# V loaded by whole batches in 32 KB descriptors, one ring of five buffers, and V's products over 128 columns of weights

## The chip, the core and the metric

The kernel runs on one core of one Trainium2 chip. The metric is the device time of one execution in microseconds (us), as the median of several executions. A profiled execution gives the trace from which the views below are taken; its span begins with the program's first instruction and ends with its last. The engines are PE (TensorE, matrix products; PEld is its loading of weights), DVE (VectorE), ACT (ScalarE), POOL (GpSimd) and SP (SyncE, which here only issues transfers). Transfers are executed by sixteen DMA engines.

## What is computed

One decoding step: a layer norm of x (8 rows of 512), attention of 32 query heads over 8 key/value heads with a window of the last 2048 keys of the caches, its output projection, and a gate from a small gated unit on the same normed rows.

```python
B, Sq, D = 8, 1, 512
Hq, Hkv, Sk, Dh = 32, 8, 8192, 128
W = min(4096, max(256, Sk // 4))                 # 2048
xn = _layernorm(x, axis=-1)
q = (xn @ wq) -> [B, Hq, 1, Dh]
k, v = the last W rows of the caches, each head serving 4 query heads
p = softmax(q @ k * Dh ** -0.5)
s = (p @ v) -> [B, Sq, Hq * Dh] @ wo
h = sigmoid(xn @ w_gate) * (xn @ w_up)           # F = 1792
return x + s * silu(h @ w_down)
```

All tensors are bf16. K and V windows have 33.5 MB each, wq and wo 4.2 MB each, the three unit weights 5.5 MB: 81 MB, of which each byte is used once.

## The kernel before

**Stages.** The query projection comes first. Then K is read in eight tiles of 4 MB (4 batches by 8 heads by 4 runs of keys make 128 partitions of 32 KB; two sets of four batches, four tiles each). VectorE transposes each K tile in place in eight pieces (L464, `k_turn`), PE makes the scores (L479, `qk`), VectorE takes row maxima (L493), ScalarE the exponentials (L507). For each set of four batches the probabilities are transposed in 32x32 blocks (L527, `soft_turn`) and spread by products with a 0/1 matrix `spread` to the partitions in which V lies (L540, `soft_spread`). VectorE then multiplies them by a 0/1 column per head (L561, `soft_mask`), so that a weight column holds only the probabilities of its own head. V's products (L609, `pv`) accumulate in PSUM; ScalarE copies the sums out (L623) and PE adds up four column groups with the 0/1 matrix `Sel` (L635, `pv_sum`), after which VectorE divides by the denominators (L644). The end is `o_rows` (L657, L664), the unit's last product `unit_out` (L381), wo's products (L723), two VectorE steps and the store.

**V.** A V tile is half a batch: 4 heads by 32 runs of 64 keys, 16 KB per partition, 2 MB, sixteen tiles. The weights of one product are 4 heads x 4 query heads x 4 column groups = 64 columns, and two products stand side by side in the two column halves of the array (`tile_position=(0, w * c)`). A tile has 16 products of 512 columns each.

**Order.** The program's order on every engine is written out by hand (`manual_schedule`). The loop at L669 runs over slots t: eight slots per K tile (piece t is transposed in slot t, its scores are in slot t+4), and from slot `PV_LAG` = 52 on V's products, four slots per V tile, beside the last K tiles' scores. `MASK_AT` sets the slots of the masks; `EXP_AT` those of the exponentials.

**Loads.** All large loads are issued from SP in one order, `loads` (L202): K0 to K6, V0, V1, K7, V2 to V13, gate and up weights, V14, V15, down weights, wo. K tiles and weights lie in a ring of 3 buffers of 32 KB per partition, V tiles in one of 4 buffers of 16 KB. A load waits for the release of its buffer, and `issue_loads` (L216) keeps the order, so that a load that waits holds up all behind it. Each transfer also waits for the completion of the eighth transfer before it, whose semaphore it uses again. wo is loaded in six pieces, so that its products can begin before it is complete.

Of the kernel before, what the change touches and what calls it, by code (L numbers as in the profile page):

```python
# [10 lines left out]
def kernel(  # L11
# [13 lines left out]
    nc = tc.nc  # L25
# [18 lines left out]
    PP = P // GL  # L44
    CH = W // PP
    NQ = P // 32
    NJ = 4
    CC = CH // NJ
    NT = B * NG
# [11 lines left out]
    VSET = NT // HB  # L61
# [14 lines left out]
    NCH = 4  # L76
    KRING = 3
    VRING = 4
    CG = CH // NCH
# [17 lines left out]
    kring = ctx.enter_context(tc.tile_pool(name="kring", bufs=KRING))  # L97
    vring = ctx.enter_context(tc.tile_pool(name="vring", bufs=VRING))
# [19 lines left out]
    def k_tile(shape, name):  # L118
        return kring.tile(shape, bf16, name=name, tag="kring", align_bytes=ALIGN)

    def v_tile(shape, name):
        return vring.tile(shape, bf16, name=name, tag="vring", align_bytes=ALIGN)
# [8 lines left out]
    wq_sb = k_tile([P, KT, Hq * Dh], "wq_sb")  # L131
# [8 lines left out]
    def load_k(i):  # L140
        hb, kq = divmod(i, NK)
        t = k_tile([P, KC, Dh], "k_sb")
# [9 lines left out]
    def v_of(i):  # L152
        hb, n = divmod(i, VSET)
        gg, q = divmod(n, NQ)
        return NQ * hb + q, gg
# [15 lines left out]
    def load_gate_up():  # L171
        t = k_tile([P, 2, KT, F], "wgu_sb")
        for n, w in enumerate((B_w_gate, B_w_up)):
            load(t[:, n], w.rearrange("(p kt) n -> p kt n", kt=KT))
            wgu_sb.append(t[:, n])

    def load_down():
        t = k_tile([P, FT, D], "wd_sb")
# [6 lines left out]
    def load_wo():  # L185
        t = k_tile([P, KW, D], "wo_sb")
# [56 lines left out]
    x_f = ppool.tile([B, D], f32, name="x_f", tag="pp")  # L243
    nc.vector.tensor_copy(out=x_f[:], in_=x_bf[:])  # L244
    stats = work.tile([B, nc.vector.BN_STATS_DIM], f32, name="stats")
    nc.vector.bn_stats(out=stats[:], in_=x_f[:])
    mv = work.tile([B, nc.vector.BN_AGGR_DIM], f32, name="mv")
    nc.vector.bn_aggr(out=mv[:], in_=stats[:])
    eps_t = work.tile([B, 1], f32, name="eps_t")
    nc.vector.memset(eps_t[:], 1e-5)  # L250
    rstd = work.tile([B, 1], f32, name="rstd")
# [19 lines left out]
    for c in range(NCOL):  # L271
# [32 lines left out]
    Hm = consts.tile([P, GL], f32, name="Hm")  # L304
    nc.vector.tensor_reduce(
        out=Hm[:],
        in_=ident[:].rearrange("p (a gl) -> p gl a", gl=GL),
# [3 lines left out]

    spread = consts.tile([P, NG, 2, PP, GL], bf16, name="spread")
    nc.gpsimd.memset(spread[:].rearrange("p a b c d -> p (a b c d)").bitcast(f32), 0.0)
    for j in range(GL):
        for gg in range(NG):
            g = NG * gg + j // 2
            nc.gpsimd.tensor_copy(
                out=spread[:, gg, j % 2, :, j], in_=ident[:, 32 * g : 32 * g + PP]
            )

    w = NCH * GL * rep
    rows_of = ppool.tile([P, w], f32, name="rows_of", tag="pp")
    nc.vector.tensor_reduce(
        out=rows_of[:],
        in_=ident[:].rearrange("p (a m) -> p m a", m=w),
        axis=AX.X,
        op=ALU.add,
    )
    Sel = consts.tile([P, NCH, GL, rep], f32, name="Sel")
    nc.vector.tensor_copy(  # L330
        out=Sel[:], in_=rows_of[:].rearrange("p (g c r) -> p c g r", g=GL, c=NCH)
    )

    NE = P // Hq
    pick = consts.tile([32 * NG, NE, P], bf16, name="pick")
    nc.gpsimd.memset(pick[:].rearrange("p e m -> p (e m)").bitcast(f32), 0.0)
    for gg in range(NG):
        rows = slice(32 * gg, 32 * (gg + 1))
        cols = slice(NE * GL * rep * gg, NE * GL * rep * (gg + 1))
        for e in range(NE):  # L340
            nc.gpsimd.tensor_copy(
                out=pick[rows, e, cols].rearrange("p (h d) -> p h d", d=NE)[:, :, e],
                in_=ident[rows, 32 * gg : 32 * gg + GL * rep],
            )
# [108 lines left out]
    o_sb = work.tile([32 * NG, B, Dh], bf16, name="o_sb")  # L453
    nc.vector.memzero(o_sb[:])
# [76 lines left out]
    def soft_spread(hb):  # L531

        pt = pt_of.pop(hb)[:].rearrange("p c (y m) -> p c y m", y=2)
        pc = ppool.tile([P, NG, NQ, CH, rep], bf16, name="pc_bf", tag="pp")
        for gg in range(NG):
            for ch in range(2):
                c = slice(CB * ch, CB * (ch + 1))
                pT_ps = psum_a.tile([P, CB, NQ, rep], f32, name="pT_ps", tag="acc_ps")
                for y in range(2):
                    nc.tensor.matmul(  # L540
                        pT_ps[:],
                        lhsT=spread[:, gg, y].rearrange("p k g -> p (k g)"),
# [4 lines left out]
                    )  # L547
                nc.scalar.copy(  # L548
                    out=pc[:, gg, :, c, :].rearrange("p q c r -> p c q r"),
# [4 lines left out]
    def soft_mask(hb, gg):  # L554

        pT_of[hb, gg] = work2.tile(
            [P, NQ * CG, GL, NCH * rep], bf16, name="pT_sb"
        )
        pc = pc_of[hb][:, gg].rearrange("p q (c e) r -> p (q c) (e r)", e=NCH)
        for gl in range(GL):  # L560
            nc.vector.tensor_scalar(  # L561
                out=pT_of[hb, gg][:, :, gl, :],
                in0=pc,
                scalar1=Hm[:, gl : gl + 1],
# [3 lines left out]

    GW = GL * rep

    def soft_den(hb):
# [8 lines left out]
        den_ps = psum1.tile([32 * NG, NQ], f32, name="den_ps", tag="misc")  # L580
        rden = small.tile([32 * NG, NQ], f32, name="rden")
        for gg in range(NG):
            rows = slice(32 * gg, 32 * gg + GW)
            nc.tensor.matmul(  # L584
                den_ps[rows, :],
                lhsT=HR[:, GL * gg : GL * (gg + 1)].rearrange("m h r -> m (h r)"),
                rhs=dq[:],
                start=True,
                stop=True,
                tile_position=(0, 32 * gg),  # L590
                skip_group_check=True,
            )
            nc.vector.reciprocal(out=rden[rows, :], in_=den_ps[rows, :])
        rden_of[hb] = rden

    def pv(t):


        i, j = divmod(t, NJ)
        b, gg = v_of(i)  # L600
        w = GL * rep * NCH
        if j == 0:
            acc_tiles[i] = psum_a.tile([P, NCH * Dh], f32, name="acc_ps", tag="acc_ps")
        q = b % NQ
        pT = pT_of[b // NQ, gg][:, CG * q : CG * (q + 1)].rearrange("p c g n -> p (c g n)")
        for n in range(CC // NCH):
            c = n % (P // w)
            ch = CC * j + NCH * n
            nc.tensor.matmul(  # L609
                acc_tiles[i][w * c : w * (c + 1), :],  # L610
                lhsT=pT[:, GL * rep * ch : GL * rep * ch + w],
                rhs=v_tiles[i][:, ch : ch + NCH, :].rearrange("p c d -> p (c d)"),
                start=(j == 0 and n < P // w),
                stop=(j == NJ - 1 and n >= CC // NCH - P // w),
                tile_position=(0, w * c),
                skip_group_check=True,
            )
        if j == NJ - 1:
            if i % NSUM == 0:
                acc_sbs[i // NSUM] = work.tile(  # L620
# [3 lines left out]
                out=acc_sbs[i // NSUM][:, i % NSUM], in_=acc_tiles.pop(i)[:]  # L624
            )

    def pv_sum(i, n):

        b, gg = v_of(i)
        q = b % NQ  # L630
        acc_sb = acc_sbs[i // NSUM][:, i % NSUM : i % NSUM + n]
        rows = slice(32 * gg, 32 * gg + GW)
        o_ps = psum1.tile([32 * NG, NSUM, Dh], f32, name="o_ps", tag="misc")
        for c in range(NCH):
            nc.tensor.matmul(  # L635
                o_ps[rows, :n, :],
                lhsT=Sel[:, c].rearrange("p g r -> p (g r)"),
# [3 lines left out]
                tile_position=(0, 32 * gg),  # L641
# [3 lines left out]
            out=o_sb[rows, b : b + n, :],  # L645
            in0=o_ps[rows, :n, :],
            in1=rden_of[b // NQ][rows, q : q + n].unsqueeze(2).to_broadcast([GW, n, Dh]),
# [21 lines left out]
    for t in range(PV_LAG + NSLOT):  # L669
# [3 lines left out]
        for hb in range(HB):  # L673
            if t == EXP_AT[hb]:
                soft_exp(hb)
            for gg in range(NG):
                if t == MASK_AT[hb, gg]:
                    soft_mask(hb, gg)
# [9 lines left out]
        if u >= NJ and u % NJ == 0:  # L688
            i = u // NJ - 1
            if i == NT - 2:  # L690
# [81 lines left out]
```

## Time and profile before

| | us |
|---|---|
| median of three executions | 197.33 |
| the executions | 197.10, 197.33, 197.42 |
| profiled execution | 197.29 |
| its span | 195.5 |

| engine | busy us | share of the span | instructions |
|---|---|---|---|
| PE | 102.9 | 53% | 750 |
| DVE | 105.5 | 54% | 149 |
| ACT | 30.8 | 16% | 69 |
| POOL | 4.6 | 2% | 25 |

| group | count | mean ns |
|---|---|---|
| L464 DVE transpose of K, 128x1024 | 64 | 1210 |
| L479 PE scores, 512 columns | 256 | 565 |
| L609 PE V's products, 512 columns | 256 | 443 |
| L561 DVE mask, 128x1024 | 16 | 477 |
| L540 PE spread, 512 columns | 16 | 501 |
| L635 PE sums of V's column groups | 48 | 477 |

How to read it: the profile's page lists the busy time of each engine, the same in 40 slices of the span (each digit is tenths), the clock that TensorE was granted (PEclk), the mean busy share of the sixteen DMA engines and the GB/s that they moved; the chain of waits, followed back from the last instruction; and groups of instructions by line and shape. Matrix products are pipelined and their ends are modelled, so the spacing of their starts says more than their length. The trace also holds each DMA packet with its size and time.

### The profile page before, as it was taken

How to read it: one execution, taken by the hardware profiler on the slowest of the kernel's cores; microseconds unless marked ns; L12 is line 12 of the kernel's file. 1: busy time of each engine (PE TensorE's matmuls, PEld its weight loads, DVE VectorE, ACT ScalarE, POOL GpSimd, SP SyncE). 2: the span in 40 equal slices, each digit the busy share in tenths (PEclk: the TensorE clock that was granted, in tenths of full speed). 3: DMA queues.
4: the chain of work that ended last, by engine and by line, in shares of the span. 5: the costliest groups of instructions: out<-in, count | busy, mean ns of one | idle time of the engine just before them, and what ended most of it. 6: DMA issues, size and time to landing. Idle time of an engine off the chain costs nothing.

```text
span 195.5 us, 1888 instructions
## 1 busy us (share of the span) xinstructions
PE 102.9 (53%) x750; PEld 36.2 (19%) x750; DVE 105.5 (54%) x149; ACT 30.8 (16%) x69; POOL 4.6 (2%) x25
## 2 busy tenths in 40 slices
PE   0062014434323258403695989858944893577763
PEld 0020001101000012100121222322311131223551
DVE  0156499999899998899969726403100010040301
ACT  2025050000000084000011143511111114010100
POOL 8000000000000000000000000000000000000000
PEclk9999999999999999955588799988999798597999
DMA  7999999999999999999999999999999999999990
GB/s 276 423 476 429 436 429 429 429 429 421 429 429 429 429 429 429 389 432 463 429 419 432 436 422 429 427 429 429 429 429 432 429 431 425 431 429 432 425 390 30
DMA packets 5128, 81.14 MB, mean 415 GB/s; under 512 B 616, under 2 KB 896, under 8 KB 1152
## 3 DMA queue, kind: packets, MB, share of 16 engines
q1 hardware_dynamic: 5056, 81.01, 97.0%
q8 instruction: 6, 0.10, 0.2%
q10 hardware_dynamic: 64, 0.01, 0.0%
q14 instruction: 2, 0.02, 0.0%
HBM read 81.01 MB, written 0.01 MB: 414 GB/s over the span
## 4 chain that ended last, share of the span: by engine, by line
DMA 62%; DVE 23%; PE 10%; issue 1%; ACT 1%; SPq 0%; DVEq 0%
DMA k_sb<-in_A_k_cache_dram 31%; DMA v_sb<-in_A_v_cache_dram 22%; DVE k_sb L464 18%; DMA wo_sb<-in_A_wo_dram 10%; PE acc_ps L609 4%; DVE pt_bf L527 2%; PE s_ps L479 2%; PE pT_ps L540 2%; PE o_ps L635 2%; DVE mx L493 1%; SPq L116 0%; DVE qz_sb L434 0%; DVE o_sb L644 0%; PE den_ps L584 0%; DVE qT_sb L424 0%
## 5 line engine op out<-in xcount | busy, mean ns | idle before, releaser
L464 DVE STREAM_TRANSPOSE k_sb<-k_sb 128x1024 f32<-128x1024 f32 x64 | 73.7, 1210 | 6.7 <-DMA k_sb<-in_A_k_cache_dram 6.6
L479 PE MATMUL s_ps<-k_sb,qz_sb 128*32 128x512 bf16 x256 | 29.8, 565 | 54.2 <-DVE k_sb L464 48.4
L609 PE MATMUL acc_ps<-v_sb,pT_sb 128*64 128x512 bf16 x256 | 39.6, 443 | 10.7 <-DMA v_sb<-in_A_v_cache_dram 10.6
L644 DVE TENSOR_TENSOR o_sb<-o_ps,rden 16x512 bf16<-16x512 f32 (+2 forms) x6 | 3.0, 504 | 47.5 <-PE o_ps L635 47.5
L479 PEld LDWEIGHTS <-qz_sb 128*32 128x32 bf16 x256 | 8.5, 116 | 78.6 <-issue 55.3
L623 ACT COPY acc_sb<-acc_ps 128x512 f32<-128x512 f32 x16 | 9.4, 586 | 84.7 <-PE acc_ps L609 84.7
L609 PEld LDWEIGHTS <-pT_sb 128*64 128x64 bf16 x256 | 13.3, 120 | 31.5 <-DMA v_sb<-in_A_v_cache_dram 14.6
L635 PE MATMUL o_ps<-acc_sb,Sel 128*16 128x512 f32 (+2 forms) x48 | 15.9, 477 | 3.4 <-ACT acc_sb L623 3.4
L561 DVE TENSOR_SCALAR pT_sb<-pc_bf,Hm 128x1024 bf16<-128x1024 bf16 x16 | 6.6, 477 | 6.7 <-PE acc_ps L609 6.7
L507 ACT ACT_TABLE_LOAD x1 | 1.3, 1283 | 39.9 <-DVE nm L501 39.9
L635 PEld LDWEIGHTS o_ps<-acc_sb,Sel 128*16 128x16 f32 x48 | 4.5, 103 | 14.9 <-issue 7.7
L493 DVE TENSOR_REDUCE mx<-s_ps 128x1 f32<-128x512 f32 x8 | 5.3, 662 | 3.2 <-PE s_ps L479 3.2
L540 PE MATMUL pT_ps<-pt_bf,spread 128*128 128x512 bf16 x16 | 6.0, 501 | 1.3 <-DVE pt_bf L527 0.7
L267 PE MATMUL xnT_ps<-ident,xn_bf 8*128 8x8 bf16 x4 | 0.3, 174 | 11.6 <-DVE xn_bf L257 11.6
L436 ACT COPY qz_sb<-qT_sb 32x32 bf16<-32x32 bf16 x20 | 4.8, 241 | 8.2 <-DVE qT_sb L424 7.9
L355 PE MATMUL d_ps<-wgu_sb,xnT_sb 128*32 128x448 bf16 x32 | 3.0, 511 | 5.3 <-DMA wgu_sb<-in_B_w_up_dram 3.0
L723 PE MATMUL a_ps<-wo_sb,o_sb 128*32 128x256 bf16 x64 | 4.5, 273 | 2.0 <-DMA wo_sb<-in_A_wo_dram 2.0
L507 ACT ACTIVATE p_bf<-s_ps,nm 128x512 bf16<-128x512 f32 x8 | 5.4, 686 | 0.0
L244 DVE CAST x_f<-x_bf 8x512 f32<-8x512 bf16 x1 | 0.4, 415 | 9.2 <-DMA x_bf<-in_A_x_dram 9.2
L548 ACT CAST pc_bf<-pT_ps 128x512 bf16<-128x512 f32 x8 | 4.5, 587 | 5.0 <-DVE pt_bf L527 2.8
L527 DVE STREAM_TRANSPOSE pt_bf<-p_bf 128x512 bf16<-128x512 bf16 x8 | 4.9, 668 | 0.0
L723 PEld LDWEIGHTS <-o_sb 128*32 128x32 bf16 x64 | 3.5, 96 | 3.1 <-issue 3.0
(59 smaller groups left out, 39.4 us busy)
## 6 DMA issues: line engine op xcount, KB each, us to landing
k_sb<-in_A_k_cache_dram SPq DMA_DIRECT2D x8, 4096.0 KB, 19.3
v_sb<-in_A_v_cache_dram SPq DMA_DIRECT2D x16, 2048.0 KB, 15.7
wq_sb<-in_A_wq_dram SPq DMA_DIRECT2D x1, 3072.0 KB, 11.4
wo_sb<-in_A_wo_dram SPq DMA_DIRECT2D x1, 2048.0 KB
wgu_sb<-in_B_w_gate_dram SPq DMA_DIRECT2D x1, 1792.0 KB
wgu_sb<-in_B_w_up_dram SPq DMA_DIRECT2D x1, 1792.0 KB, 24.7
wd_sb<-in_B_w_down_dram SPq DMA_DIRECT2D x1, 1792.0 KB
wq_sb<-in_A_wq_dram SPq DMA_DIRECT2D x1, 1024.0 KB, 4.6
```

What stands on the lines that cost most here:

```text
L436: nc.scalar.copy(out=out, in_=in_)
L464: nc.vector.transpose(out=kw, in_=kw)
L479: nc.tensor.matmul(s_tiles[i][32 * g : 32 * (g + 1), :], lhsT=qz_sb[:, hb, h, 2 * a + e, :], rhs=kT[:, :, a, h, :, e], start=(n == 0), sto ...
L493: nc.vector.reduce_max(out=mx_of[hb][:, kq : kq + 1], in_=s_tiles[i][:], axis=AX.X)
L507: nc.scalar.activation(out=p_bf[:, :, kq], in_=s_tiles.pop(NK * hb + kq)[:].rearrange("p (o c j) -> p c j o", o=2, j=NC), func=AF.Exp, bia ...
L527: nc.vector.transpose(out=pt[:, w * n : w * (n + 1)], in_=p_bf[:, w * n : w * (n + 1)])
L540: nc.tensor.matmul(pT_ps[:], lhsT=spread[:, gg, y].rearrange("p k g -> p (k g)"), rhs=pt[:, c, y, :], start=(y == 0), stop=(y == 1), skip_ ...
L561: nc.vector.tensor_scalar(out=pT_of[hb, gg][:, :, gl, :], in0=pc, scalar1=Hm[:, gl : gl + 1], scalar2=None, op0=ALU.mult,)
L609: nc.tensor.matmul(acc_tiles[i][w * c : w * (c + 1), :], lhsT=pT[:, GL * rep * ch : GL * rep * ch + w], rhs=v_tiles[i][:, ch : ch + NCH, : ...
L623: nc.scalar.copy(out=acc_sbs[i // NSUM][:, i % NSUM], in_=acc_tiles.pop(i)[:])
L635: nc.tensor.matmul(o_ps[rows, :n, :], lhsT=Sel[:, c].rearrange("p g r -> p (g r)"), rhs=acc_sb[:, :, Dh * c : Dh * (c + 1)], start=(c == 0 ...
L723: nc.tensor.matmul(a_ps[32 * c : 32 * (c + 1), :], lhsT=o2_sb[:, k, :], rhs=wo_parts[k][:, DC * c : DC * (c + 1)], start=(k == 0), stop=(k ...
```

## The change

- **V's layout and loads.** A V tile is a whole batch: 8 heads by 16 runs of 128 keys (`RUNS`, `CV`), 32 KB per partition, 4 MB, eight tiles. It is loaded by two transfers of 2 MB: heads 0 to 3 into the even partitions, heads 4 to 7 into the odd ones. The last tile is loaded in two column halves, so by four transfers of 1 MB.
- **One ring.** K tiles, V tiles and weights share one ring of 5 buffers of 32 KB per partition (before: 3 x 32 KB and 4 x 16 KB, the same memory). A load waits for the release of the fifth load before it. The order is K0 to K6, V0, K7, V1 to V6, gate and up weights, V7, down weights, wo.
- **wo's pieces** are of 12, 9, 5, 3, 2 and 1 rows in place of 16, 8, 4, 2, 1 and 1.
- **V's products.** The weights of one product have 8 heads x 4 x 4 = 128 columns; 32 products per batch, eight slots of four. The count stays at 256.
- **Masks.** One call per batch, 8 heads, 128x512 each: 64 in place of 16 of 128x1024. Batches 0 and 1 are masked at the slots of before; batch b from 2 on when batch b-2 has been multiplied (two buffers `pT_sb`).
- **Sums.** `pv_sum` adds up batches 0 to 3, then 4 to 6 (between the two halves of the last batch), then 7. All 32 query heads lie in one block of rows, so `o_sb`, `den_ps`, `rden` and `pick` have 32 rows in place of 64, and the denominators take one product and one reciprocal per set in place of two.
- **x** is loaded by two transfers in place of three, and the small tiles of the layer norm are columns of one tile.

```diff
-    PP = P // GL
+    PP = 32
     CH = W // PP
-    NJ = 4
-    CC = CH // NJ
-    NT = B * NG
+    RUNS = P // Hkv
+    CV = W // RUNS
+    NCH = 4
+    CG = CV // NCH
+    NJ = 8
+    CGJ = CG // NJ
+    NT = B
...
-    MASK_AT = {}
-    for gg in range(NG):
-        MASK_AT[0, gg] = EXP_AT[0] + 9 + gg
-        MASK_AT[1, gg] = max(EXP_AT[1] + 6, PV_LAG + NJ * NQ * (gg + 1))
+    MASK_AT = {0: EXP_AT[0] + 9, 1: EXP_AT[0] + 10}
+    for b in range(2, NT):
+        MASK_AT[b] = PV_LAG + NJ * (b - 1)
-    KRING = 3
-    VRING = 4
+    RING = 5
...
-    for c0, c1 in ((0, 2), (2, 3), (3, 4)):
+    for c0, c1 in ((0, 2), (2, 4)):
...
-    def load_v(i):
-        b, gg = v_of(i)
-        t = v_tile([P, CH, Dh], "v_sb")
-        load(
-            t[:].rearrange("p c d -> p (c d)"),
-            A_v_cache[b, GL * gg : GL * (gg + 1), win0:Sk, :].rearrange(
-                "j (p c) d -> p j (c d)", c=CH
-            ),
-        )
-        v_tiles[i] = t
+    v_runs = A_v_cache[:, :, win0:Sk, :].rearrange(
+        "b h (k c) d -> b k h (c d)", c=CV
+    )
+
+    def load_v(b):
+        t = big([P, CV, Dh], "v_sb")
+        flat = t[:].rearrange("p c d -> p (c d)")
+        parts = 2 if b == NT - 1 else 1
+        n = CV * Dh // parts
+        for h in range(parts):
+            cols = slice(n * h, n * (h + 1))
+            for a in range(2):
+                load(flat[a::2, cols], v_runs[b, :, GL * a : GL * (a + 1), cols])
+        v_tiles[b] = t
...
-            (0, 16),
-            (16, 24),
-            (24, 28),
-            (28, 30),
-            (30, 31),
+            (0, 12),
+            (12, 21),
+            (21, 26),
+            (26, 29),
+            (29, 31),
             (31, 32),
...
-    loads[-2:-2] = [(2, 0)]
+    loads[-1:-1] = [(2, 0)]
     loads = loads + [(2, 1), (2, 2)]
-    k_order = [(4, 0)] + [x for x in loads if x[0] != 1]
-    v_order = [x for x in loads if x[0] == 1]
+    order = [(4, 0)] + loads
...
-            order, n = (v_order, VRING) if kind == 1 else (k_order, KRING)
-            at = order.index(x)
-            if at >= n and order[at - n] not in released:
+            at = loads_done[0] + 1
+            if at >= RING and order[at - RING] not in released:
                 break
...
+    spread = consts.tile([P, 2, 2, P], bf16, name="spread")
+    for o in range(2):
+        for y in range(2):
             nc.gpsimd.tensor_copy(
+                out=spread[:, o, y].rearrange(
+                    "p (k i s a) -> p s a i k", i=2, s=2, a=2
+                )[:, y],
+                in_=ident[:].rearrange("p (a i k o) -> p o a i k", a=2, i=2, o=2)[:, o],
+            )
...
+    def soft_mask(b):
+
+        pT_of[b] = work2.tile([P, CG, Hkv, NCH * rep], bf16, name="pT_sb")
+        pc = pc_of[b // NQ][:, b % NQ].rearrange("p (c e) r -> p c (e r)", e=NCH)
+        for h in range(Hkv):
             nc.vector.tensor_scalar(
+                out=pT_of[b][:, :, h, :],
                 in0=pc,
+                scalar1=Hm[:, h : h + 1],
                 scalar2=None,
                 op0=ALU.mult,
             )
...
+        b, j = divmod(t, NJ)
+        if j == 0:
+            acc_tiles[b] = psum_a.tile([P, NCH * Dh], f32, name="acc_ps", tag="acc_ps")
+        for cg in range(CGJ * j, CGJ * (j + 1)):
             nc.tensor.matmul(
+                acc_tiles[b][:],
+                lhsT=pT_of[b][:, cg].rearrange("p h n -> p (h n)"),
+                rhs=v_tiles[b][:, NCH * cg : NCH * (cg + 1), :].rearrange(
+                    "p c d -> p (c d)"
+                ),
+                start=(cg == 0),
+                stop=(cg == CG - 1),
                 skip_group_check=True,
             )
...
-        if u >= NJ and u % NJ == 0:
-            i = u // NJ - 1
-            if i == NT - 2:
-                pv_sum(i, 1)
-            elif i == NT - 3:
-                pv_sum(i - 1, 2)
-            elif i % NSUM == NSUM - 1:
-                pv_sum(i + 1 - NSUM, NSUM)
+        if u == NJ * NSUM:
+            pv_sum(0, NSUM)
+        elif u == NSLOT - NJ // 2:
+            pv_sum(NSUM, NT - NSUM - 1)
...
-        if u == NSLOT - 2 * NJ - 1:
+        if u == NSLOT - NJ - 1:
             unit_in(wgu_sb[0])
             unit_in(wgu_sb[1])
             released.add((2, 0))
             issue_loads()
-        if u == NSLOT - 2 * NJ:
+        if u == NSLOT - NJ:
             unit_mid()
```

More of the change, by code (lines that the diff above doesn't have):

```diff
@@ L60 @@
     SET = NK * KTS
-    VSET = NT // HB
     QK_LAG = 4
@@ L116, in load, with big @@
         q.dma_start(out=dst, in_=src)
[L118 to L122, printed above, removed]
+    def big(shape, name):
+        return ring.tile(shape, bf16, name=name, tag="ring", align_bytes=ALIGN)
     x_bf = work.tile([B, D], bf16, name="x_bf")
-    for c0, c1 in ((0, 2), (2, 3), (3, 4)):
+    for c0, c1 in ((0, 2), (2, 4)):
         nc.scalar.dma_start(
@@ L302 @@
     )
-    Hm = consts.tile([P, GL], f32, name="Hm")
+    Hm = consts.tile([P, Hkv], f32, name="Hm")
     nc.vector.tensor_reduce(
         out=Hm[:],
-        in_=ident[:].rearrange("p (a gl) -> p gl a", gl=GL),
+        in_=ident[:].rearrange("p (a h) -> p h a", h=Hkv),
         axis=AX.X,
@@ L310 @@
     )
[L312 to L316, printed above, removed]
+    spread = consts.tile([P, 2, 2, P], bf16, name="spread")
+    nc.gpsimd.memset(spread[:].rearrange("p a b c -> p (a b c)").bitcast(f32), 0.0)
+    for o in range(2):
+        for y in range(2):
             nc.gpsimd.tensor_copy(
-                out=spread[:, gg, j % 2, :, j], in_=ident[:, 32 * g : 32 * g + PP]
-            )
[L321 to L332, printed above, removed]
+                out=spread[:, o, y].rearrange(
+                    "p (k i s a) -> p s a i k", i=2, s=2, a=2
+                )[:, y],
+                in_=ident[:].rearrange("p (a i k o) -> p o a i k", a=2, i=2, o=2)[:, o],
+            )
+    Sel = consts.tile([P, NCH, Hkv, rep], f32, name="Sel")
+    for a in range(2):
+        nc.vector.tensor_copy(
+            out=Sel[:, :, GL * a : GL * (a + 1), :],
+            in_=ident[:].rearrange("p (i a c r) -> p a c i r", a=2, c=NCH, r=rep)[:, a],
+        )
     NE = P // Hq
-    pick = consts.tile([32 * NG, NE, P], bf16, name="pick")
+    pick = consts.tile([Hq, NE, P], bf16, name="pick")
     nc.gpsimd.memset(pick[:].rearrange("p e m -> p (e m)").bitcast(f32), 0.0)
[L337 to L344, printed above, removed]
+    for e in range(NE):
+        nc.gpsimd.tensor_copy(
+            out=pick[:, e, :].rearrange("p (h d) -> p h d", d=NE)[:, :, e],
+            in_=ident[:Hq, :Hq],
+        )
     FQ = F // 4
@@ L452 @@
     acc_sbs = {}
-    o_sb = work.tile([32 * NG, B, Dh], bf16, name="o_sb")
-    nc.vector.memzero(o_sb[:])
+    o_sb = work.tile([Hq, B, Dh], bf16, name="o_sb")
     def k_turn(t):
@@ L533, in soft_spread @@
         pt = pt_of.pop(hb)[:].rearrange("p c (y m) -> p c y m", y=2)
-        pc = ppool.tile([P, NG, NQ, CH, rep], bf16, name="pc_bf", tag="pp")
-        for gg in range(NG):
+        pc = ppool.tile([P, NQ, CV, rep], bf16, name="pc_bf", tag="pp")
+        for o in range(2):
             for ch in range(2):
@@ L547, in soft_spread @@
                     )
+                cv = slice(CH * o + CB * ch, CH * o + CB * (ch + 1))
                 nc.scalar.copy(
-                    out=pc[:, gg, :, c, :].rearrange("p q c r -> p c q r"),
+                    out=pc[:, :, cv, :].rearrange("p q c r -> p c q r"),
                     in_=pT_ps[:],
@@ L579, in soft_den @@
         )
[L580 to L593, printed above, removed]
+        den_ps = psum1.tile([Hq, NQ], f32, name="den_ps", tag="misc")
+        rden = small.tile([Hq, NQ], f32, name="rden")
+        nc.tensor.matmul(
+            den_ps[:],
+            lhsT=HR[:].rearrange("m h r -> m (h r)"),
+            rhs=dq[:],
+            start=True,
+            stop=True,
+        )
+        nc.vector.reciprocal(out=rden[:], in_=den_ps[:])
         rden_of[hb] = rden
     def pv(t):
-        i, j = divmod(t, NJ)
-        b, gg = v_of(i)
-        w = GL * rep * NCH
+        b, j = divmod(t, NJ)
         if j == 0:
[L603 to L615, printed above, removed]
+            acc_tiles[b] = psum_a.tile([P, NCH * Dh], f32, name="acc_ps", tag="acc_ps")
+        for cg in range(CGJ * j, CGJ * (j + 1)):
+            nc.tensor.matmul(
+                acc_tiles[b][:],
[5 more added lines that the diff above has]
+                stop=(cg == CG - 1),
                 skip_group_check=True,
@@ L618, in pv @@
         if j == NJ - 1:
-            if i % NSUM == 0:
-                acc_sbs[i // NSUM] = work.tile(
+            if b % NSUM == 0:
+                acc_sbs[b // NSUM] = work.tile(
                     [P, NSUM, NCH * Dh], f32, name="acc_sb"
@@ L623, in pv, with pv_sum @@
             nc.scalar.copy(
-                out=acc_sbs[i // NSUM][:, i % NSUM], in_=acc_tiles.pop(i)[:]
+                out=acc_sbs[b // NSUM][:, b % NSUM], in_=acc_tiles.pop(b)[:]
             )
-    def pv_sum(i, n):
-        b, gg = v_of(i)
+    def pv_sum(b, n):
         q = b % NQ
-        acc_sb = acc_sbs[i // NSUM][:, i % NSUM : i % NSUM + n]
-        rows = slice(32 * gg, 32 * gg + GW)
-        o_ps = psum1.tile([32 * NG, NSUM, Dh], f32, name="o_ps", tag="misc")
+        acc_sb = acc_sbs[b // NSUM][:, b % NSUM : b % NSUM + n]
+        o_ps = psum1.tile([Hq, NSUM, Dh], f32, name="o_ps", tag="misc")
         for c in range(NCH):
             nc.tensor.matmul(
-                o_ps[rows, :n, :],
-                lhsT=Sel[:, c].rearrange("p g r -> p (g r)"),
+                o_ps[:, :n, :],
+                lhsT=Sel[:, c].rearrange("p h r -> p (h r)"),
                 rhs=acc_sb[:, :, Dh * c : Dh * (c + 1)],
@@ L644, in pv_sum @@
         nc.vector.tensor_tensor(
-            out=o_sb[rows, b : b + n, :],
-            in0=o_ps[rows, :n, :],
-            in1=rden_of[b // NQ][rows, q : q + n].unsqueeze(2).to_broadcast([GW, n, Dh]),
+            out=o_sb[:, b : b + n, :],
+            in0=o_ps[:, :n, :],
+            in1=rden_of[b // NQ][:, q : q + n].unsqueeze(2).to_broadcast([Hq, n, Dh]),
             op=ALU.mult,
@@ L675 @@
                 soft_exp(hb)
-            for gg in range(NG):
-                if t == MASK_AT[hb, gg]:
-                    soft_mask(hb, gg)
+        for b in range(NT):
+            if t == MASK_AT[b]:
+                soft_mask(b)
         if t < KSLOT:
```

43 lines of the change are left out of this document (14 added, 29 removed).

## The prediction

> **What bounds the kernel now.** First the share of the DMA engines over the span in forty slices, and the bytes they moved:
>
> ```profile
> DMA  7999999999999999999999999999999999999990
> GB/s 276 423 476 429 436 429 429 429 429 421 429 429 429 429 429 429 389 432 463 429 419 432 436 422 429 427 429 429 429 429 432 429 431 425 431 429 432 425 390 30
> q1 hardware_dynamic: 5056, 81.01, 97.0%
> ```
>
> The engines are full from the second slice to the last but one; 389 beside 463 is a packet counted in the neighbouring slice, since the row above shows no hole. Sixteen engines are occupied for 97% of 195.5 us. The totals by stage ask whether K and V run at different rates (columns: window, length, PE, PEld, DVE, ACT, POOL busy, PEclk, DMA share, GB/s):
>
> ```profile
> 15.00:62.00 47.00, 14.16 (x123) 4.18 (x113) 41.77 (x51) 5.41 (x21) 0.00 (x0) 1.00 1.00 431
> 104.00:157.00 53.00, 39.52 (x228) 12.23 (x228) 15.95 (x28) 11.22 (x23) 0.00 (x0) 0.90 1.01 430
> ```
>
> The first window moves K alone (32 KB packets), the second V and at its end weights (16 KB). The rates agree within 1 GB/s. VectorE is nearly full in the first, and neither VectorE nor TensorE in the second. Then the end of the chain of waits (start, length, what), and PE late in the timeline:
>
> ```profile
> 147.14 25.99 DMA v_sb<-in_A_v_cache_dram
> 173.13 0.02 issue
> 173.15 18.96 DMA wo_sb<-in_A_wo_dram
> 192.11 0.04 issue
> 192.15 0.30 PE a_ps L723 x2
> 192.45 0.02 issue
> 192.47 0.42 DVE prod L734
> ```
> ```profile
> 178.03 3.56 PE L609 MATMUL acc_ps<-v_sb,pT_sb 128*64 128x512 bf16 x16 [1.21 <-DMA v_sb<-in_A_v_cache_dram]
> 181.62 0.59 ACT L623 COPY acc_sb<-acc_ps 128x512 f32<-128x512 f32 x1 [5.90 <-PE acc_ps L609]
> 184.21 1.71 PE L381 MATMUL b_ps<-wd_sb,hT_sb 128*32 128x256 bf16 x28
> 187.12 1.92 PE L723 MATMUL a_ps<-wo_sb,o_sb 128*32 128x256 bf16 x32 [1.21 <-DMA wo_sb<-in_A_wo_dram]
> ```
>
> The stream ends with wo at 192.11; two small products, two VectorE steps and the store close the span 3.4 us later. PE has done everything but wo's products at 185.92 and then waits for wo. So the time is start-up, plus what sixteen engines need for 81 MB, plus a fixed end. A change counts only if it shortens the packets' total, leaves the engines without work, or makes the end later than wo's last byte.
>
> **Packets (the gain).** In the trace's packet records the median packet takes 1.213 us for 32,768 bytes, 0.611 for 16,384, 0.309 for 8,192, 0.159 for 4,096, 0.084 for 2,048, 0.046 for 1,024. Doubling a size costs about 8 ns less than twice, so a packet costs bytes at a steady pace plus 7 to 9 ns. V now: 16 tiles x 128 packets / 16 engines = 128 packets per engine x 0.611 = 78.2 us. After: seven batches x 8 packets x 1.213 = 67.9, and the last batch in halves, 16 x 0.611 = 9.8; sum 77.7. Gain 0.5 us. wo stays at six packets per partition of 32 KB in all, so its total stays (1.255 us before, 1.254 after, x8). Two more DMAs add two 9 ns completion packets per engine; one x load less takes one away on another queue. Total: -0.5 us.
>
> **The unknown in it.** Every large transfer in this trace writes all 128 partitions. A write to 64 partitions two apart, fed from 16 runs by 4 heads, does not occur. The work divides evenly (64 packets, 4 per engine). On the memory side K's 32 heads by 4 runs and V's old 32 runs by 4 heads cost the same per byte, so the order of addresses has made no difference here. Ends: the 32 KB packet costs 1.213 as for K, or at worst 1.762, the slowest one on record: 64 x 0.549 = +35 us. I take 1.213: size and engine load are K's, and 1.762 happened twice in 1,024. In between, a run of about 25 K packets at 47 to 53 us took 1.25 to 1.34.
>
> **The ring (0).** Each load now waits for the release of the fifth before it. A full tile streams in 8 x 1.213 = 9.7 us, so loads start at about 51 (K4), 61, 70, 80 (V0), 90 (K7), 100 (V1) and so on. SP's issues today show when K0 to K4 came free: 34.98, 44.58, 54.19, 64.64, 79.59. K7 follows K3: free at 65, due at 90. V1 follows K4: 80 against 100. V5 follows K7, free about 121 (next paragraph), due 139. The least slack I find is 17 us, where a load is queued far ahead. A transfer also waits for the eighth before it (today's last wo piece was issued at 173.15, when V14 landed); after, the last wo piece waits for V7's third of four pieces, with 7 MB, 16 us, still queued. Behind a held transfer stand all later ones, but the queue in front is never empty. Without this cover each late microsecond would be one lost.
>
> **VectorE's masks (0).** Sixteen of 128x1024 at 477 ns (7.6 us) become 64 of 128x512. Bounds for one: 150 ns (the 128x1 TENSOR_SCALAR of L501) and 477; midway about 310, so 20 us, 12 more. Within K's stage: 16 masks x 0.31 = 5.0 against 8 x 0.46 = 3.7, and a third batch's 2.5 us ahead of K7's last four transposes, which waits for V0's products. Behind it stand those transposes, and behind them PE's scores. PE also executes V1's products between K7's scores, so K's stage ends when V1 (landing near 110) has been multiplied, near 121 instead of 114.9. Exponentials, transposes and spread took about 9 us after that, so masks for V4 are there by 135 to 141; V4 lands near 139, and being a few us late there only eats the releases' slack.
>
> **V's products (0).** 256 products stay 256, but they no longer run as pairs in two column halves. Pairs start 0.213 to 0.236 us apart at full clock, 0.427 at half. A batch takes 32 x 0.213 = 6.8 us (8.6 at 0.27, the 128-column products of L540), under the 9.7 us in which it arrives; at half clock 13.7 us, over it. Adding 27 us of work to a PE that was half idle also keeps it busier. The set sums of L635 (8 x 0.43 us) and weights fit the 2.9 us left per batch, once with a few us of lag.
>
> **The end (0, narrowly).** V7's first half lands about 172.6, its second 177.5. PE: 16 x 0.213 = 3.4; the sum over three batches, 8 x 0.43 x 3/4 = 2.6; 16 more, 3.4: done at 182.0, later than today's 181.59. From there today's rows need 4.33 us to the end of L381, then 31 rows of wo at 0.105 (L723's spacing): 189.6, ahead of the last byte at 192.1 - 0.5 = 191.6. One half-clock window costs 1 us, two about 2.7, and then it is late.
>
> Sum: 197.29 - 0.5 = **196.8** (span 195.0, and 1.78 around it as now). The profiled 197.29 lies within 0.04 of the median, 197.33.
>
> **Rivals.** (a) *The 64-partition transfers are slower.* Place: V's packets, 77.7 us of stream with nothing to hide behind. It decides from 1.221 us per packet (the gain gone). For it: no row shows this shape. Against: equal bytes and packets per engine, and address orders that did not matter. At 1.30, the middle of the disturbed run, 64 x 0.087 = +5.6, or 202.4 us; at 1.762, 232. If two engines had to take turns at one entrance of the on-chip memory for all of V, packets would take 2.43 and the time would be 274.
>
> [...]
>
> (b) *PE becomes late at the end.* Two half-clock windows at V7: wo's products done at about 192.3 instead of 191.6, so 196.8 + 0.7 = 197.5. For it: today's 178.03 row shows 16 products at half clock (3.56 us; 1.92 at full), after idle gaps, and PE waits 3.5 us for V7 after the gate products. Against: it is busier before.
>
> (c) *It does nothing.* Larger packets don't shorten the stream, if the 8 ns are hidden between packets: 197.3. The two windows above, 431 against 430, can't exclude it.
>
> **Chances.** Forecast 0.50, (a) 0.20, (b) 0.18, (c) 0.12. A measurement here tells about 0.2% (0.4 us); the gain is 0.25%, so some of the forecast reads as no change: 0.38 faster, 0.12 same. (b): 0.04, 0.08, 0.06. (c): 0.02, 0.10, 0. (a) is all slower. Sums: faster 0.44, same 0.30, slower 0.26. Range: low 196.2, the forecast less twice the 0.3 by which the three runs spread; high 199.2, V's packets at 1.25, the mild end of the disturbed run, 64 x 0.037 = 2.4. The rest of (a) is left out. Forecast, (b) and (c) alone: 196.4 to 197.7.
>
> **What would show it.** Right: V's 32 KB packets at 1.213, packets down by about 900, no hole in the DMA row, wo's last byte near 191.6 and PE waiting for it. (a): GB/s below 425 in V's slices. (b): PE's wo products back to back to the end, no wait for wo. Ring wrong: a DMA digit under 9 between 50 and 180 us. What would overturn it is any idle DMA time in V's stage.

## The result and the profile after

The changed kernel takes 277.75 us (four executions, 275.89 to 279.64) against 197.36 us before; the ratio is 1.408, 95% interval 1.398 to 1.417. The profiled span is 276.0 us.

The page of the changed kernel, share of the DMA engines and bytes moved in forty slices of 6.9 us, and the queue of the large loads:

```profile
DMA  8999999999999999999999999999999989999980
GB/s 317 444 427 408 456 443 401 442 456 389 451 375 211 204 313 408 223 223 199 199 223 226 223 223 220 204 204 223 230 215 218 218 198 422 247 242 247 392 368 19
q1 hardware_dynamic: 4192, 81.01, 97.0%
```

The engines are as full as before, 97% of the span, and move the same 81.01 MB in fewer packets (4192; before 5056). But where V streams they move about 215 GB/s in place of 430. The dip at the 13th and 14th slice is V0, the 15th and 16th hold K7, at 408 in the second of them, then come V1 to V6. The totals by stage of the same kernel, K alone and V alone (window, length, busy time and count of PE, PEld, DVE, ACT, POOL, then PEclk, DMA share, GB/s):

```profile
15.00:62.00 47.00, 14.22 (x124) 4.18 (x116) 41.48 (x50) 5.39 (x21) 0.00 (x0) 0.55 1.00 432
110.00:200.00 90.00, 50.97 (x210) 17.36 (x206) 23.78 (x56) 7.77 (x17) 0.00 (x0) 0.77 1.00 216
```

K at 432, V at 216, both with every engine occupied. TensorE's granted clock in K's stage, 0.55 beside 1.00 before, has no part in this: K streams at 432 all the same. A busy DMA engine is therefore not an engine that moves data at its pace: its packets simply take longer. The packet records say by how much:

```
packets of the changed kernel          count   mean us   the same size before
32 KB, 15 to 75 us (K)                   784     1.215   1.213 median (K)
32 KB, 110 to 230 us (V1 to V6)          756     2.425   no V packet of this size
16 KB, 230 to 270 us (V7)                257     1.114   0.611 median (V)
```

2.425 is twice 1.213. V7's packets, in the shorter transfers at the end, vary more, from 0.63 to 1.33 us. The end of the chain of waits of the changed kernel:

```profile
249.46 22.64 DMA wo_sb<-in_A_wo_dram
272.10 0.04 issue
272.14 0.62 PE a_ps L690 x6
272.76 0.02 issue
272.78 0.42 DVE prod L701
```

As before, the stream's last bytes are wo's and the same short tail follows. The whole loss is in the stream: 64 packets of V per engine at 1.21 us more would be 78 us, and the span grew by 80.5.

Two groups of the page, for the steps on PE and VectorE:

```profile
L582 PE MATMUL acc_ps<-v_sb,pT_sb 128*128 128x512 bf16 x256 | 76.1, 457 | 71.6 <-DMA v_sb<-in_A_v_cache_dram 71.6
L546 DVE TENSOR_SCALAR pT_sb<-pc_bf,Hm 128x512 bf16<-128x512 bf16 x64 | 17.4, 342 | 48.0 <-PE acc_ps L582 48.0
```

PE is idle ahead of V's products for 71.6 us (10.7 before), all of it waiting for V's loads. A mask takes 342 ns in the mean, and VectorE is busy with masks for 17.4 us in all.

### The profile page after: what moved, and what is told of

Same layout as the page of the kernel before. It is cut to its first block, busy times and chain, and to the rows that moved or that the text cites. A ratio compares the mean times of both kernels' runs of the same rounds, so it can differ in the third digit from the quotient of the medians.

```text
span 276.0 us, 1857 instructions
## 1 busy us (share of the span) xinstructions
PE 129.3 (47%) x722; PEld 46.9 (17%) x722; DVE 113.5 (41%) x191; ACT 26.1 (9%) x61; POOL 4.1 (1%) x17
## 3 DMA queue, kind: packets, MB, share of 16 engines
q1 hardware_dynamic: 4192, 81.01, 97.0%
HBM read 81.01 MB, written 0.01 MB: 294 GB/s over the span
## 4 chain that ended last, share of the span: by engine, by line
DMA 44%; another core or an unknown queue 37%; PE 10%; DVE 5%; SPq 3%; issue 1%; ACT 0%; ACTq 0%
DMA k_sb<-in_A_k_cache_dram 35%; DMA wo_sb<-in_A_wo_dram 8%; PE acc_ps L582 7%; DVE k_sb L450 5%; SPq L114 3%; PE s_ps L465 2%; PE pT_ps L526 1%; PE a_ps L690 0%; ACT pc_bf L535 0%; DVE mx L479 0%; DVE prod L701 0%; DVE y_bf L703 0%; PE den_ps L565 0%; ACTq L535 0%
## 5 line engine op out<-in xcount | busy, mean ns | idle before, releaser
L582 PE MATMUL acc_ps<-v_sb,pT_sb 128*128 128x512 bf16 x256 | 76.1, 457 | 71.6 <-DMA v_sb<-in_A_v_cache_dram 71.6
L582 PEld LDWEIGHTS <-pT_sb 128*128 128x128 bf16 x256 | 26.8, 112 | 115.8 <-issue 98.7
L546 DVE TENSOR_SCALAR pT_sb<-pc_bf,Hm 128x512 bf16<-128x512 bf16 x64 | 17.4, 342 | 48.0 <-PE acc_ps L582 48.0
L597 ACT COPY acc_sb<-acc_ps 128x512 f32<-128x512 f32 x8 | 4.7, 586 | 163.1 <-PE acc_ps L582 163.1
L615 DVE TENSOR_TENSOR o_sb<-o_ps,rden 32x512 bf16<-32x512 f32 (+2 forms) x3 | 1.5, 501 | 22.1 <-PE o_ps L607 22.1
L358 DVE TENSOR_TENSOR h_sb<-sig,d_ps 128x448 bf16<-128x448 f32 x1 | 0.6, 621 | 20.5 <-PE d_ps L342 20.5
L607 PE MATMUL o_ps<-acc_sb,Sel 128*32 128x512 f32 (+2 forms) x24 | 7.4, 453 | 1.4 <-ACT acc_sb L597 1.4
L392 PE MATMUL q_ps<-wq_sb,xnT_sb 128*32 128x512 bf16 x32 | 3.8, 626 | 1.7 <-DMA wq_sb<-in_A_wq_dram 1.7
```

What stands on the lines that cost most here:

```text
L546: nc.vector.tensor_scalar(out=pT_of[b][:, :, h, :], in0=pc, scalar1=Hm[:, h : h + 1], scalar2=None, op0=ALU.mult,)
L582: nc.tensor.matmul(acc_tiles[b][:], lhsT=pT_of[b][:, cg].rearrange("p h n -> p (h n)"), rhs=v_tiles[b][:, NCH * cg : NCH * (cg + 1), :].re ...
L607: nc.tensor.matmul(o_ps[:, :n, :], lhsT=Sel[:, c].rearrange("p h r -> p (h r)"), rhs=acc_sb[:, :, Dh * c : Dh * (c + 1)], start=(c == 0), ...
```

## The experiments

Three theories for packets that take twice as long, 2.425 us in place of 1.213. All three are suppositions to be tested; no record shows an entrance of the memory. Theory 1: with 16 runs each of the 16 engines takes one run, that is eight neighbouring partitions of the tile (four of them per transfer), and engines whose partitions lie 32 apart write through one entrance of the on-chip memory at the same moment, and must take turns. Theory 2: a transfer into alternate partitions reaches only half of the entrances. Theory 3: the order of addresses in memory is slow.

The packet records give size and time but not the engine, so which engine writes which partitions is inferred from the runs, not seen. e5, e6 and e9 are medians of 12, 11 and 11 executions; every other run is one execution.

**One transfer in place of two (e1).**

```diff
-            for a in range(2):
-                load(flat[a::2, cols], v_runs[b, :, GL * a : GL * (a + 1), cols])
+            load(flat[:, cols], v_runs[b, :, :, cols])
...
```

> The changed kernel with one V transfer per batch (16 runs by 8 heads into all 128 partitions, heads in order; spread and Sel follow). Theory 1 (each engine takes one run, so eight neighbouring partitions, and engines four apart write at the same entrance at the same time): V's packets still 2.4 us, about 275 us. Theory 2 (a transfer into 64 partitions two apart reaches half the entrances): packets 1.21, about 197 us. Theory 3 (runs 32 KB apart of heads 2 MB apart are read slowly): 2.4 us, about 275 us.

It took 292.19 us. The totals by stage:

```profile
120.00:200.00 80.00, 38.72 (x148) 13.22 (x152) 21.73 (x52) 6.59 (x15) 0.00 (x0) 0.71 1.01 212
```

All 128 partitions in one transfer are no cure: 212 GB/s, packets of 2.5 us. Theory 2 falls. It is 14 us over the changed kernel. By the packet records some 10 us of that are longer packets, per engine: 5.4 in those of 32 KB (V's take 2.50 us in the mean from 110 to 230 us, in place of 2.425), 2.0 in V7 and 2.9 in the three unit weights. The other 4 us are time in which some engines had no packet. Why these packets are longer stays open.

**Alternate partitions on the kernel before (e2).**

```diff
...
+        for a in range(2):
+            load(flat[a::2, :], src[:, a::2, :])     # 32 runs by 2 heads
```

> The kernel before, each V tile by two transfers of 32 runs by 2 heads into even and odd partitions (16 KB packets as before). Theory 1: with 32 runs over 16 engines the split is that of the old transfers, which do not meet: packets 0.61 us, about 197.5 us. Theory 2: packets 1.21 us, V takes 78 us more, about 275 us. Theory 3: addresses as before, about 197.5 us.

It took 197.50 us beside 197.35 on the same chip:

```profile
104.00:157.00 53.00, 37.77 (x227) 12.52 (x228) 15.81 (x28) 10.96 (x23) 0.00 (x0) 0.94 1.01 430
```

The same 64 alternate partitions, filled from 32 runs by 2 heads, take the full 430 GB/s. Neither the 64 partitions nor their spacing costs anything here. What is left is 32 runs or 16, and the size of a packet, which e3 leaves at 16 KB.

**Two halves on the kernel before (e3).**

```diff
...
+        for a in range(2):
+            load(flat[64 * a : 64 * (a + 1), :], src[16 * a : 16 * (a + 1), :, :])
```

> The kernel before, each V tile by two transfers of 16 runs by 4 heads into the lower and the upper 64 neighbouring partitions. Theory 1: each engine takes one run, four neighbouring partitions, and runs eight apart lie 32 partitions apart; slow if partitions 32 apart share an entrance (packets 1.2 us, about 275 us), fast if not. Theory 2 (only alternate partitions are the trouble): about 197.5 us. Theory 3: addresses as before, about 197.5 us.

It took 279.50 us:

```profile
120.00:200.00 80.00, 38.88 (x184) 11.48 (x184) 13.05 (x25) 9.53 (x20) 0.00 (x0) 0.69 1.01 217
```

217 GB/s again, with the old packet size and addresses. Here one run is four partitions, and runs eight apart lie 32 partitions apart. The kernel before, with the size and products it always had, becomes as slow as the changed one by this edit alone. The run has a second reading, which stays open: the lower 64 partitions may have only half of the entrances however they are filled, and no run fills 64 neighbouring partitions from 32 runs. Theory 1 does not hang on it, since e1 and e5 (below) set 16 rows against 32 in all 128 partitions, and the changed kernel and e2 do so in alternate ones.

**Addresses alone (e4).**

```diff
-            A_v_cache[b, GL * gg : GL * (gg + 1), win0:Sk, :].rearrange(
-                "j (p c) d -> p j (c d)", c=CH
-            ),
+            A_v_cache[b, GL * gg : GL * (gg + 1), Sk - 2 * W : Sk, :].rearrange(
+                "j (p two c) d -> two p j (c d)", two=2, c=CH
+            )[0],
```

> The kernel before with the old V transfers (32 runs by 4 heads, 128 partitions, 16 KB packets), but runs 32 KB apart in memory: it reads the first half of each 32 KB of the last 4096 keys, so the keys are others than the reference's. Theory 1 and 2: nothing changes, about 197.4 us. Theory 3: packets about 1.2 us and about 275 us.

It took 197.39 us, with the full rate in the same window:

```profile
104.00:157.00 53.00, 39.73 (x229) 12.20 (x228) 15.96 (x28) 11.34 (x23) 0.00 (x0) 0.90 1.01 431
```

Theory 3 falls.

**Eight runs, close together and spread out (e7, e10).** Both are the kernel before with four transfers per V tile.

```diff
 # e7
...
+        for a in range(4):
+            load(flat[32 * a : 32 * (a + 1), :], src[8 * a : 8 * (a + 1), :, :])
 # e10
...
+        for a in range(4):
+            p0 = 64 * (a // 2) + a % 2
+            load(flat[p0 : p0 + 63 : 2, :], src[8 * a : 8 * (a + 1), :, :])
```

> The kernel before, each V tile by four transfers of 8 runs by 4 heads into 32 neighbouring partitions. Theory 1, with as many engines as runs: eight engines, each at an entrance of its own: 16 KB packets take 0.61 us as before, but only eight are in flight, so V takes 78 us more: about 275 us. If instead all sixteen engines share the work and meet: sixteen in flight, packets 1.2 us, about 275 us too.

> As e7, eight runs by 4 heads per transfer, but into partitions two apart over 64 (the rows land in other partitions than the products expect, so the output is not the reference's). Theory 1: eight engines, of which those four apart write 32 partitions apart and meet: packets of 16 KB take 1.22 us with eight in flight, V takes 4 x 78 us, about 430 us. If partitions 32 apart do not share an entrance: packets 0.61 us and about 299 us as e7.

They took 299.40 and 319.71 us. First e7's stages, then e10's: V0's first 5 us, and the middle of V.

```profile
80.00:85.00 5.00, 1.05 (x16) 0.42 (x17) 4.97 (x9) 0.00 (x0) 0.00 (x0) 0.84 0.51 216
150.00:200.00 50.00, 22.71 (x100) 7.88 (x100) 4.42 (x12) 5.19 (x9) 0.00 (x0) 0.69 0.51 215
```
```profile
80.00:85.00 5.00, 1.72 (x16) 0.59 (x17) 4.97 (x8) 0.00 (x0) 0.00 (x0) 0.72 0.55 141
150.00:200.00 50.00, 29.56 (x134) 8.79 (x132) 8.72 (x21) 8.26 (x18) 0.00 (x0) 0.76 0.51 215
```

A DMA share of 0.51 is what eight engines of sixteen give when always busy: presumably eight engines work a transfer of eight runs, one run each. Both kernels read the same rows in the same order and differ in the destination alone. In e7 the partitions of the runs begin four apart, and V0's packets of these 5 us all take 0.611 us. In e10 they begin eight apart, so that pairs lie 32 apart, and V0 starts at 141 GB/s in place of 216, with packets of 1.02 us in the mean. So the place of the writes alone makes packets longer here, 1.02 us in place of 0.611; what the engines read is the same. e10 has spacings of 40 to 56 partitions as well, which were not tried alone, so it is not shown that the 32 are what counts.

Both expected times are misses. e10 was expected at 430 us, but its mean packets fall to 0.75 us at 125 to 130 us and to 0.61 from 145 us on, until the gate and up weights join at 230 us. A reading that fits, not a shown one, is that the pairs get out of step, and that engines which never write at the same place together lose nothing: the meeting would be a matter of time as well as of place. e8 tests it. e7 was expected at 275 us and took 24 more. From 110 to 200 us its packets take 0.612 us in the mean, as expected; where other loads stream beside V they do not. K7's packets take 2.47 us in the mean at 85 to 90 us, and V's own 1.18 at 220 to 230 us, beside the gate and up weights.

**Out of step on purpose (e8).** The changed kernel with two small transfers between K7 and V1, meant to load the engines unequally.

```diff
...
+        load(dst[0:96, :], src[0:12])      # 12 rows x 8 pieces of 8 KB
+        load(dst[96:128, :], src[12:16])   # 4 rows x 8 pieces
```

> The changed kernel with two more transfers between K7 and V1, into memory that is overwritten later: 12 rows of 8 pieces of 8 KB, then 4 rows of 8. If a transfer of 12 rows uses engines 0 to 11 and one of 4 rows engines 0 to 3, engines 0 to 3 start V1 4.9 us late, 4 to 11 2.5 us and 12 to 15 at once, and engines four apart are two packets out of step. Theory 1: they then write at different entrances, V1 to V6 take 1.21 us per packet, and the time falls to between 205 and 225 us (V0 and perhaps V7 still slow). Any theory by which the shape of the transfer or the addresses are slow in themselves: packets stay at 2.4 us and the time grows by 3 to 5 us to about 281 us.

It took 268.93 us, less than the changed kernel although it moves 1 MB more:

```profile
130.00:150.00 20.00, 11.69 (x61) 3.62 (x63) 5.26 (x12) 1.52 (x4) 0.00 (x0) 0.75 1.01 329
170.00:185.00 15.00, 12.93 (x50) 4.72 (x49) 3.51 (x12) 1.17 (x2) 0.00 (x0) 1.00 0.99 368
```

The same two windows of the changed kernel:

```profile
130.00:150.00 20.00, 12.89 (x60) 3.58 (x60) 4.09 (x13) 3.28 (x9) 0.00 (x0) 0.76 0.99 212
170.00:185.00 15.00, 12.96 (x40) 4.47 (x40) 2.19 (x8) 0.59 (x1) 0.00 (x0) 0.79 0.99 214
```

Same transfers of V, same addresses, same partitions, but 329 and later 368 GB/s in place of 212 and 214; the 32 KB packets take 1.56 us in the mean from 130 to 190 us. A theory by which shape or addresses are slow in themselves has no room for that. The time is outside my 205 to 225. The packets did not fall to 1.21, which by theory 1 means engines out of step in part only, and from 190 to 205 us the rate is back at 200 GB/s. There the gate and up weights stream beside V, and their 14 KB packets take 1.05 to 1.16 us in the mean (190 to 210 us) in place of 0.535; that they meet V's packets is the likely reason, not a shown one.

**The change with K's pattern of loads (e5, e6).** V tiles are read as K tiles are, 32 rows (batch and head) by 4 runs. The tiles then hold V's rows in another order than the products expect, so the output is not the reference's.

```diff
-            for a in range(2):
-                load(flat[a::2, cols], v_runs[b, :, GL * a : GL * (a + 1), cols])
+            k0 = win0 + NC * KC * (b % NK)
+            load(
+                flat[:, cols],
+                A_v_cache[NQ * (b // NK) : NQ * (b // NK + 1), :, k0 : k0 + NC * KC, :].rearrange(
+                    "b h (j c) d -> (b h) j (c d)", c=KC
+                )[:, :, cols],
+            )
 # e6 also
-        parts = 2 if b == NT - 1 else 1
+        parts = 2
```

> The changed kernel, but V tiles are read in K's pattern (4 batches by 8 heads by 4 runs, one transfer into 128 partitions, 32 KB packets), so the tiles hold V's rows in another order and the output is not the reference's; ring, masks, products and sums are the change's. Theory 1 (only the meeting of engines at an entrance costs): 196.8 us, packets 1.21 us, end set by wo. Rival: the late end of PE or the ring costs something as well: over 197.3 us.

> As e5, with every V tile read in two column halves, so in 16 KB packets. If a packet costs 8 to 10 ns beside its bytes: 7 batches x 8 x 9 ns = 0.5 us more than e5. Rival (c): no difference.

e5 took 197.62 us (ratio to before 1.0021, interval 1.0004 to 1.0038), e6 198.14 (1.0032, 1.0016 to 1.0048). The 80 us are gone with the pattern of the loads: ring, masks, products and layout account for none of them. V's 32 KB packets take 1.213 us, and the row of e5's DMA share has no hole:

```profile
DMA  7999999999999999999999999999999999999990
```

Last byte of wo, from the packet records: before 191.81, e5 191.37, e6 191.72. So 32 KB packets seem to shorten the stream, by 0.44 us against the kernel before and 0.34 against e6. These are single executions: e9 below, with e5's loads, has its last byte at 191.50, 0.13 later. The medians of e5 and e6 lie 0.52 apart, about the 0.5 expected, but their intervals overlap. Yet e5's median is no better than before, over the 197.3 of the rival in its expectation, and its timeline of PE says why:

```profile
172.88 5.30 PE L587 MATMUL acc_ps<-v_sb,pT_sb 128*128 128x512 bf16 x15 [4.00 <-DMA v_sb<-in_A_v_cache_dram]
178.11 2.77 PE L612 MATMUL o_ps<-acc_sb,Sel 128*32 128x384 f32 x8
180.81 3.63 PE L587 MATMUL acc_ps<-v_sb,pT_sb 128*128 128x512 bf16 x16
...
188.60 3.66 PE L695 MATMUL a_ps<-wo_sb,o_sb 128*32 128x256 bf16 x64
```

wo's 64 products run in one piece, without a wait for wo, from 188.60 to 192.26, past wo's last byte. PE idled 4.00 us before V7, and the first half's products then took 5.3 us where 16 at full clock take 3.6 (the third row). The clock over that stretch in e5:

```profile
174.00:178.00 4.00, 4.00 (x13) 1.41 (x11) 0.00 (x0) 0.00 (x0) 0.00 (x0) 0.66 0.99 419
```

0.66 of full speed. This profile is of one of e5's fastest executions (197.13; they range from 197.11 to 198.61). The profile of e6 is of its slowest, 198.68. There PE is at half clock from 168.73 to 178.97 us by the clock records, and wo's products end at 193.73:

```profile
172.00:179.00 7.00, 5.58 (x13) 2.11 (x15) 0.00 (x0) 0.00 (x0) 0.00 (x0) 0.50 1.00 423
190.07 3.66 PE L695 MATMUL a_ps<-wo_sb,o_sb 128*32 128x256 bf16 x64
```

So how late PE ends seems to vary with the clock from one execution to the next.

**The sum moved (e9).** As e5, with the sum over batches 4 to 6 ahead of the last batch.

```diff
-        elif u == NSLOT - NJ // 2:
+        elif u == NSLOT - NJ:
             pv_sum(NSUM, NT - NSUM - 1)
```

> As e5 (tiles hold V's rows in another order), with the sum over batches 4 to 6 moved from between the two halves of the last batch to ahead of them, right behind the gate products, where PE waits for V7 anyway. Theory (e5's end is set by PE: 16 products at half clock, then the sum, then 16 more): PE has wo's products done as they land, the last byte of wo at 191.4 sets the end, span 194.9 and median 196.8 us. Rival (the end is set by something else, or the earlier sum delays other work): no change against e5, 197.6 us.

e9 took 197.02 us against 197.37 (ratio 0.9984, interval 0.9975 to 0.9993). Its PE timeline:

```profile
168.84 2.74 PE L612 MATMUL o_ps<-acc_sb,Sel 128*32 128x384 f32 x8
172.92 3.61 PE L587 MATMUL acc_ps<-v_sb,pT_sb 128*128 128x512 bf16 x16 [1.34 <-DMA v_sb<-in_A_v_cache_dram]
177.76 3.61 PE L587 MATMUL acc_ps<-v_sb,pT_sb 128*128 128x512 bf16 x16 [1.23 <-DMA v_sb<-in_A_v_cache_dram]
...
191.54 0.61 PE L695 MATMUL a_ps<-wo_sb,o_sb 128*32 128x256 bf16 x6 [0.17 <-DMA wo_sb<-in_A_wo_dram]
```
```profile
174.00:178.00 4.00, 2.77 (x14) 1.19 (x13) 0.00 (x0) 0.00 (x0) 0.00 (x0) 1.00 1.00 424
```

The sum fills the gap, PE keeps its full clock (1.00 where e5 had 0.66), both halves take 3.61 us, and wo's last products wait for wo again. The result is 0.2 us beside the expected 196.8.

A kernel that computes the reference with V in this row order would need its probabilities spread by batch, head and run, and its products split by batch. It wasn't built. The 0.16% of e9 is what it could win over the kernel before, as an estimate that takes these changes to cost nothing.

## Why the prediction was wrong

**The step that failed** is the one called the unknown: "I take 1.213: size and engine load are K's". Size and load were indeed K's. What differs is the number of rows. K and the old V have 32 rows of runs or heads for 16 engines, and ran at 430 GB/s; with 16 rows, so presumably one per engine, e1, e3 and the change ran at 212 to 217. That pairs of engines then meet where they write is the reading that fits these runs; no record shows it. Measured: 2.425 us in place of 1.213 from V1 to V6. Against e5, which has the same packet sizes, the 32 KB packets took 213.9 us per engine in place of 145.8 and V7's of 16 KB 17.8 in place of 9.8, 76 us more in all. My upper bound, the slowest packet on record (1.762; it happened once, the other one was 1.744), was no bound either: it came from transfers of 32 rows, and says nothing of those of 16.

**Rival (a)** was the true one in its time, though not because of the 64 partitions, which e2 fills at 430 GB/s. Its case of two engines that take turns at one entrance for all of V gave packets of 2.43 and 274 us; 2.425 and 277.75 came. The factor of two was my estimate; that there is such an entrance no run shows. I gave it a chance of 0.20, priced it at 1.30 and 1.762 as well, and left all but its mildest case out of the range. Equal bytes per engine and an indifference to addresses, which I counted against it, do not bear on it: they concern the load of an engine and the reading side, while e7 and e10 read the same rows, differ in the destination alone, and begin V0 at 216 and 141 GB/s.

Theory 1 is borne out in part. e3 (217 GB/s), e10 (141 against e7's 216) and the factor of two agree with it; which engines meet, and where, is not shown. One transfer into 128 partitions in place of two would not have helped (e1, 292.19 us), and on the kernel before two transfers in place of one changed little (e2, 197.50 beside 197.35).

**Packets (-0.5 us): right in size** by single profiles, -0.44 by e5's last byte and -0.34 between e6 and e5 (e9: -0.31 and -0.22). **The ring (0): right.** The DMA row of e5 has no hole, and its stream ends earlier, not later. **Masks (0): right**; one takes 0.34 us in place of the estimated 0.31, and e5's chain of waits holds none. **V's products (0): right**; 16 take 3.61 us at full clock, which is 0.216 apart plus the last one's length.

**The end (0, narrowly): wrong, by rival (b).** The step had wo's products done at 189.6, ahead of wo's last byte, at full clock throughout. In e5 PE idled 4.00 us before V7, the clock was at half from 173.35 to 176.76 us by the clock records, and wo's products ended at 192.26. The price of such a window was too low: I had put it at 1 us, but the first half's products took 5.30 us against 3.61 in e9, so 1.7. So even at K's packet rate the forecast of 196.8 would have been missed: 197.62. That rival (b) said 197.5 is in part luck, since it had two windows at 2.7 us, and e5's profile, of a faster execution, shows one. e9 agrees: with the sum ahead of V7 the clock stays at 1.00 from 174 to 178 us, where e5 had 0.66, and the ratio to before goes from 1.0021 to 0.9984. In the changed kernel itself this end is hidden: V is so late that wo's products wait for wo.

## What to carry to other kernels

Before splitting a load, ask how many rows it has for the engines and which partitions they may write at the same time, not only how many bytes each gets: with as many rows as engines (16 runs) packets took 2.425 us, which is read here as engines meeting in pairs; with 32 rows the same bytes into the same partitions took 1.213 (e5). A DMA share of 97%, the same before and after, says nothing of this; the duration of a packet of known size does, and GB/s by stage shows it (430 and 216). And where an engine has just been given more work near the end, put its sums into its waits, ahead of the late data, so that they do not stand behind it: e9 took 0.9984 of the time before, e5 1.0021.

## What was not expected of the hardware

In e10 the slowdown ended by itself: with eight runs V's packets went from 1.02 us at 80 us to 0.61 at 145 us, by way of 1.45 while K7 streamed beside them, and stayed at 0.61 until the weights joined at 230 us. With sixteen (the changed kernel) they stayed at 2.40 to 2.44 in the mean of every 5 us from 110 to 225 us. With two small unequal transfers ahead of them (e8) the same V transfers went from 212 and 214 to 329 and 368 GB/s, but from 190 to 205 us, beside the weights, the rate was 200 again. That engines fall out of step, or stay in step, is the reading that fits all three; the records don't show it directly.
